# Order of early work in a local and pooled attention kernel with a cosine-gated FFN: loads, banks, sums of keys, and the first part of the passes

## The chip, the cores and the metric

The kernel runs on one core of a Trainium2 chip. Its engines are TensorE (PE in the profile; its weight loads are PEld), VectorE (DVE), ScalarE (ACT), GpSimd (POOL) and SyncE (SP, which issues most DMAs). SBUF holds tiles of 128 partitions, PSUM has eight banks that take matmul results. The metric is the device time of one execution in microseconds, less is better.

## The reference

Eight batches of eight heads with 576 tokens of width 64. Each head gets two attentions, which are added; then an FFN with `h * cos(h)` follows.

```python
q_d = q.reshape(B, H, Sd, factor, D).mean(axis=3)     # k_d, v_d alike; factor 4
out_up = np.repeat(sm_attn(q_d, k_d, v_d), factor, axis=2)
mask = np.abs(pos[:, None] - pos[None, :]) < factor
scores = np.where(mask, scale * np.matmul(q, k.transpose(0, 1, 3, 2)), -1000000000.0)
attn = softmax(scores)
out_local = np.matmul(attn, v)
x = (out_up + out_local).transpose(0, 2, 1, 3).reshape(B * S, H * D)
h = x @ w_in
g = h * np.cos(h)
return g @ w_out
```

`x` has 4608 rows of 512; `w_in` is 512 x 2048 and `w_out` 2048 x 512, both handed over in 64-bit floats, as two 32-bit words each.

## The kernel before

**Units.** Attention is done by pairs of heads: four pairs (`pr`) to a batch, 32 in all. A pair has five parts. `u_qk` loads q and k and sums them in groups of four tokens (`qkd`). `u_v` loads v twice, for the pooled attention (`vd4`, summed to `vd`) and for the local one (`vl`). `u_s` makes the scores on TensorE (L501 local, L509 pooled), masks them, takes maxima, exponentials and sums, and divides. `u_t` transposes the weights (L578, L589), and `u_pv` multiplies with the values (L606, L617), adds both attentions on VectorE (L625, the tile `xs`), and writes the result as a high and a low part (`x0h`, `x0l`, and so on) into x tiles of 384 tokens.

**FFN.** The tokens are 12 x tiles, d_ff is 16 chunks of 128. A step is one tile and one chunk: `gemm1` (12 matmuls, L668), an elementwise chain on ScalarE and VectorE whose first VectorE instruction is L680 and whose second is L683, and two steps later `gemm2` (9 matmuls, L704). There are 192 steps. `PASSES` gives their order: the first three tiles come with chunks 0 to 7, then the same three with chunks 8 to 15, then nine tiles with all chunks. The second part adds to the first in DRAM through GpSimd's DMA queue.

**Weights.** `w_load` brings a chunk of `w_in` or `w_out` as words (`wdi`, `wdo`, 512 KB each), and `w_split` makes a high and a low part: ScalarE L400, four VectorE instructions L401, L403, L405, L407 on a staging tile (`xxh` or `xxl`, with three places each), ScalarE's L411 and a subtraction (L379, on GpSimd or VectorE). 32 such splits are needed.

**Borrowed room.** The first two batches are early (`NEARLY`). Three of their four pairs work in the buffers of weight chunks 8 to 15 (`wx`, named wxi and wxo in the profile; `OWN` tells which); those chunks are loaded when the pairs are done. The last x tile lends the staging tiles.

**Order.** Nothing is placed by hand. `at(t, f, ...)` gives each part a due time, each operation has an estimated cost, and `Plan.schedule` lists the operations forwards and backwards over several rounds and keeps the best. Where an operation may run on two engines (`alts`), the planner picks one. Each engine then executes its own list in order. Where TensorE is expected to idle, matmuls on an identity (L806) are put in as filler. Early sums of keys (`ON_PE = (1,)`) are four matmuls with an identity (L455) and a copy (L440, L441); sums of queries are reductions on VectorE (L465) or three additions on GpSimd (L458, L460). `bank` gives the parts of batch 0 all eight banks; batch 1 uses the ring of three that the later batches use.

## Time and profile before

| | us |
|---|---|
| median of three runs | 1049.72 (1047.09 to 1053.25) |
| profiled execution | 1051.08 |
| its span | 1048.9 |
| TensorE busy in the span | 1015.9 |
| VectorE busy | 670.1 |
| ScalarE busy | 616.5 |
| GpSimd busy | 218.3 |

The profile cuts the span in 40 slices of 26.2 us and writes each engine's busy share in tenths. A line of a group or of the timeline names the engine, the source line, the operation and the tiles (result `<-` operands), then durations, and behind `<-` what ended the idle time ahead of it. A busy TensorE need not be at its peak, since matmuls overlap and filler counts as work. DMA moved 71.43 MB in the span.

### The profile page before, as it was taken

Reading aid. Unit: us, or ns where it says so; the run is one execution under the profiler, and the core shown is the slowest. Engines: PE = TensorE matmul, PEld = TensorE weight load, DVE = VectorE, ACT = ScalarE, POOL = GpSimd, SP = SyncE. Lnnn points to the kernel's source line nnn. Section 1 sums busy time; section 2 is a strip of 40 time slices with the busy share of each in tenths; the row PEclk is TensorE's granted clock in tenths of the full one; section 3 lists DMA queues with packets and bytes.
Section 4 is the critical chain, followed back from the end, with each engine's and each line's share of the span. In section 5 each row is a group of like instructions: output and inputs, shape, how many; then the busy total and the mean of one; then the engine's idle time right before and its main releaser. Section 6 shows DMA issues by size and latency. Waiting matters only on the chain.

```text
span 1048.9 us, 26356 instructions
## 1 busy us (share of the span) xinstructions
PE 1015.9 (97%) x11316; PEld 895.1 (85%) x11316; DVE 670.1 (64%) x1378; ACT 616.5 (59%) x1185; POOL 218.3 (21%) x225
## 2 busy tenths in 40 slices
PE   7987898999999999999999999999999999999998
PEld 6776787798888888888898888888898888899997
DVE  4698999964668766654647856745545964534433
ACT  2475776755566665665656755646656665555554
POOL 3557645311123211100102210300010210000000
PEclk8699899999999999999999999999999999999999
DMA  8385550002232411200102410300100410000000
GB/s 249 129 250 160 177 193 12 31 31 44 65 82 73 112 46 50 81 24 28 54 28 70 119 43 24 108 24 27 54 28 24 131 55 1 31 1 1 31 1 31
DMA packets 33861, 71.43 MB, mean 68 GB/s; under 512 B 3152, under 2 KB 11344, under 8 KB 33744
## 3 DMA queue, kind: packets, MB, share of 16 engines
q1 hardware_dynamic: 32448, 67.38, 20.5%
q0 software_dynamic: 1296, 2.36, 1.6%
q8 instruction: 89, 1.46, 0.6%
q14 instruction: 28, 0.23, 0.1%
HBM read 57.93 MB, written 11.80 MB: 66 GB/s over the span
## 4 chain that ended last, share of the span: by engine, by line
PE 82%; DVE 11%; issue 2%; DMA 2%; ACT 1%; POOL 0%; SPq 0%; ACTq 0%; POOLq 0%; DVEq 0%
PE bank L704 34%; PE bank L668 33%; PE bank L617 4%; PE bank L501 3%; PE bank L509 2%; PE bank L606 2%; PE bank L589 2%; PE bank L455 1%; DMA wdi<-w_in 1%; PE bank L578 1%; PE bank L806 1%; DMA q<-qT 1%; DVE gl L379 1%; DVE tr L680 1%; DVE xxl L405 1%
## 5 line engine op out<-in xcount | busy, mean ns | idle before, releaser
L704 PE MATMUL bank<-wo,gh 128*128 128x512 f32 x1152 | 366.8, 399 | 0.6 <-DVE ob L721 0.6
L704 PEld LDWEIGHTS bank<-wo,gh 128*128 128x128 f32 x1152 | 210.0, 189 | 37.1 <-issue 3.3
L704 PE MATMUL bank<-wo,gl 128*128 128x512 f32 x576 | 228.9, 398 | 0.9 <-DVE gl L379 0.9
L683 DVE SCALAR_TENSOR_TENSOR tr<-tr,bank 128x384 f32<-128x384 f32 x192 | 105.6, 550 | 130.4 <-ACT tr L678 130.2
L679 ACT ACTIVATE tr<-bank,bmagic 128x384 f32<-128x384 f32 x192 | 110.8, 577 | 123.8 <-PE bank L668 116.7
L680 DVE SCALAR_TENSOR_TENSOR tr<-tr,bank 128x384 f32<-128x384 f32 x192 | 105.7, 551 | 101.5 <-ACT tr L679 101.4
L677 ACT ACTIVATE tr<-tr 128x384 f32<-128x384 f32 x192 | 100.8, 525 | 94.7 <-DVE tr L680 93.9
L685 ACT ACTIVATE gh<-tr 128x384 fp32r<-128x384 f32 x171 | 89.6, 524 | 104.9 <-DVE tr L683 103.5
L379 DVE TENSOR_TENSOR gl<-tr,gh 128x384 fp32r<-128x384 f32 x157 | 96.7, 616 | 72.8 <-ACT gh L685 71.1
L704 PEld LDWEIGHTS bank<-wo,gl 128*128 128x128 f32 x576 | 108.6, 189 | 25.8 <-DVE gl L379 1.7
L668 PE MATMUL bank<-x1h,wi 128*128 128x384 f32 x384 | 108.0, 342 | 3.4 <-DVE tr L683 3.4
L668 PE MATMUL bank<-x0h,wi 128*128 128x384 f32 x384 | 108.4, 343 | 1.5 <-DVE tr L683 1.5
L668 PE MATMUL bank<-x2h,wi 128*128 128x384 f32 x384 | 106.8, 338 | 0.9 <-DVE tr L683 0.9
L668 PE MATMUL bank<-x3h,wi 128*128 128x384 f32 x384 | 107.1, 339 | 0.0
L678 ACT ACTIVATE tr<-tr 128x384 f32<-128x384 f32 x192 | 100.9, 526 | 6.1
L379 POOL TENSOR_TENSOR gl<-tr,gh 128x384 fp32r<-128x384 f32 x35 | 38.1, 1090 | 317.8 <-DVE gh L686 256.9
L668 PEld LDWEIGHTS bank<-x1h,wi 128*128 128x128 f32 x384 | 70.9, 190 | 6.7 <-DVE tr L683 4.7
L668 PEld LDWEIGHTS bank<-x0h,wi 128*128 128x128 f32 x384 | 70.9, 190 | 4.8 <-DVE tr L683 2.4
L668 PEld LDWEIGHTS bank<-x2h,wi 128*128 128x128 f32 x384 | 70.2, 188 | 3.5 <-DVE tr L683 1.4
L668 PEld LDWEIGHTS bank<-x3h,wi 128*128 128x128 f32 x384 | 70.2, 188 | 2.3 <-issue 0.4
L668 PE MATMUL bank<-x1l,wi 128*128 128x384 f32 x192 | 65.0, 339 | 0.0
L668 PE MATMUL bank<-x0l,wi 128*128 128x384 f32 x192 | 64.9, 338 | 0.0
(190 smaller groups left out, 1513.1 us busy)
## 6 DMA issues: line engine op xcount, KB each, us to landing
...
```

The source lines that it names most:

```text
L379: f = lambda e: lambda: e.tensor_tensor(out=out(), in0=in0(), in1=in1(), op=ALU.subtract)
L501: pe.matmul(banks[h].get()[BS * i:BS * (i + 1), LQ + BS * s:LQ + BS * (s + 1)], q.get()[hs, o:o + BS], k.get()[hs, o:o + BS], start=True, ...
L509: pe.matmul(banks[h].get()[:HD, i * SD:(i + 1) * SD], qkd.get()[hs, 0, i * HD:(i + 1) * HD], qkd.get()[hs, 1, :], start=True, stop=True)
L617: pe.matmul(banks[e].get()[64 * h:64 * h + 64, o:o + BQ], vt.get()[r, a, i, :], ptl.get()[r, a, i, :], start=True, stop=True)
L668: pe.matmul(ph.get()[:, :m], w[:, i, kc, :], x[:, kc, :], start=(n == 0), stop=(n == 3 * KC - 1))
L677: act.activation(tr.get(), tr.get(), AF.Sin, scale=PI)
L678: act.activation(tr.get(), tr.get(), AF.Square)
L679: pl.op("ACT", _act(m, True, 1), lambda: act.activation(tr.get(), h(), AF.Identity, bias=bmagic), r=[ph], w=[tr])
L680: pl.op("DVE", _dve(m), lambda: dve.scalar_tensor_tensor(out=tr.get(), in0=tr.get(), scalar=MAGIC, in1=h(), op0=ALU.subtract, op1=ALU.subt ...
L683: pl.op("DVE", _dve(m), lambda: dve.scalar_tensor_tensor(out=tr.get(), in0=tr.get(), scalar=0.5, in1=h(), op0=ALU.subtract, op1=ALU.mult), ...
L685: pl.op("ACT", _act(m, False), lambda: act.activation(gh.get(), tr.get(), AF.Copy), r=[tr], w=[gh], alts=[("DVE", _dve(m / 2), lambda: dve ...
L704: pe.matmul(o, (gh, gh, gl)[k].get()[:, sl], wo.get()[:, (0, 1, 0)[k]], start=(c == c0 and k == 0), stop=(c == c1 - 1 and k == 2))
```

## The change

1. `PASSES` has chunks 0 to 3 (`NF = 4`) in the first part on three tiles, then chunks 4 to 15.
2. `ON_PE = ()`: early sums of keys are made as the sums of queries are, on VectorE or GpSimd.
3. Batch 1 uses all eight banks as batch 0 does, its parts are due earlier, and batches 0 and 1 get a lead of 100 and 60 us in the planner's keys (`BOOST`).
4. A chain of dependencies puts the loads of the two batches and of all weights into one order. Queries and keys of batch 1's pairs get buffers of their own (in `xxl` and in chunks 6 to 8).
5. For that, `w_split` stages in `xxh` alone, with three places.
6. The sums of both softmaxes lie in one tile `su`, so that the small addition and the reciprocal are one instruction each for both; GpSimd sets `su` to one first.

```diff
-PASSES = [(t, 0, NC // 2) for t in range(3)] + [(t, NC // 2, NC) for t in range(3)] + [(t, 0, NC) for t in range(3, NT)]
+NF = 4
+PASSES = [(t, 0, NF) for t in range(3)] + [(t, NF, NC) for t in range(3)] + [(t, 0, NC) for t in range(3, NT)]
-ON_PE = (1,)
+ON_PE = ()
+BOOST = {0: 100.0, 1: 60.0}
...
-            span, rev = self.run({o: -o.fin for o in self.ops}, True)
-            key = {o: (1 - CFG["mix"]) * (span - o.fin) + CFG["mix"] * key[o] for o in self.ops}
+            span, rev = self.run({o: o.boost - o.fin for o in self.ops}, True)
+            key = {o: span - o.fin - o.boost for o in self.ops}
...
-    for c in range(NC - 8, NC):
+    for c in range(NC - 10, NC):
...
-        v = cut(xx[nstage[0] % 2], DM * (nstage[0] // 2 % 3), [P, DM])
+        v = cut(xx[0], DM * (nstage[0] % 3), [P, DM])
...
+        if b == 1 and pr and name in "qk":
+            own = cut(xx[1], 584 * (name == "k"), shape) if pr == 1 else \
+                cut(wx[{(2, "q"): ("o", 8), (2, "k"): ("i", 7), (3, "q"): ("o", 7), (3, "k"): ("o", 6)}[(pr, name)]], 0, shape)
+            return own
...
-        if b == 0:
+        if b < NEARLY:
...
-            pl.op("DVE", 0.1, lambda su=su: dve.tensor_scalar(out=su.get(), in0=su.get(), scalar1=1e-9, scalar2=2.0 * PI,
-                                                              op0=ALU.add, op1=ALU.mult), w=[su])
-            pl.op("DVE", 0.15, lambda su=su: dve.reciprocal(su.get(), su.get()), w=[su])
+        pl.op("DVE", 0.1, lambda: dve.tensor_scalar(out=su.get(), in0=su.get(), scalar1=1e-9, scalar2=2.0 * PI,
+                                                    op0=ALU.add, op1=ALU.mult), r=[su2], w=[su])
+        pl.op("DVE", 0.15, lambda: dve.reciprocal(su.get(), su.get()), w=[su])
...
-            t = need[c] if c < NC // 2 else NC // 2 + 2.0 * (c - NC // 2)
+            t = need[c] if c < NF else NF + c - NF
...
-        for t, f in ((-4.0 + 0.5 * i, u_qk), (-2.4 + 0.5 * i, u_v), (0.1 + 1.5 * i, u_s), (1.4 + 1.5 * i, u_t), (2.7 + 1.5 * i, u_pv)):
+        for t, f in ((-7.9 + 0.5 * i, u_qk), (-4.4 + 0.5 * i, u_v), (-3.4 + i, u_s), (-2.4 + i, u_t), (-1.4 + i, u_pv)):
             at(t, f, 1, i)
...
+    chain = [o for k in ul("u_qk", 0) + ul("u_v", 0) + ul("u_qk", 1) + wl(0) + ul("u_v", 1) + wl(*range(1, NC))
+             for o in loads[k]]
+    for o, n in zip(chain, chain[1:]):
+        n.sdeps.append(o)
```

In the changed kernel the line numbers shift: L501 becomes L513, L509 L521, L578 L595, L589 L606, L606 L623, L617 L634, L625 L642, L668 L685, L680 L697, L683 L700, L704 L721, L806 L835, L379 L386, the split's L400 to L411 become L407 to L418.

What the planner makes of it is seen at three places. On TensorE, at the start, behind the first filler (k and q are pair 0 of batch 0; wxo_120 and wxi_151 hold pair 1), before:

```order
L455 MATMUL bank<-k,ident 128x144 x4
L501 MATMUL bank<-k,q 32x32 x48
L509 MATMUL bank<-qkd 72x144 x4
L455 MATMUL bank<-wxo_120,ident 128x144 x4
L501 MATMUL bank<-wxo_120,wxi_151 32x32 x48
L509 MATMUL bank<-wxi_151 72x144 x4
L455 MATMUL bank<-wxi_208,ident 128x144 x4
L455 MATMUL bank<-wxo_211,ident 128x144 x4
```

and in the changed kernel, a little later, from the fourth pair's scores (wxo_287 and wxi_230) through the first pair's transposes and product with the values to the second pair's transpose:

```order
L513 MATMUL bank<-wxo_287,wxi_230 32x32 x48
L521 MATMUL bank<-wxi_230 72x144 x4
L595 MATMUL bank<-ident,sml 128x128 x3
L606 MATMUL bank<-ident,smd 72x72 x8
L634 MATMUL bank<-ptl,vl 64x24 x48
L623 MATMUL bank<-ptd,vd 64x144 x4
L595 MATMUL bank<-ident,wxi_291 128x128 x3
```

The matmuls with keys are gone, and pairs follow each other without them. On SyncE, from the loads that follow those of batch 0, before:

```order
L390 DMA wdi_544<-w_in 128x4x256 [waits DMAHW0_49]
L390 DMA wdo_613<-w_out 128x1024 [waits DMAHW1_49]
L451 DMA q<-qT 128x584 [waits DMAHW2_49,DVE_49,PE_49]
L451 DMA wxo_120<-kT 128x584 [waits DMAHW3_49,PE_49,Activation_49]
L390 DMA wdi_729<-w_in 128x4x256 [waits DMAHW4_49]
L451 DMA k<-kT 128x584 [waits DMAHW5_49]
L451 DMA wxi_208<-kT 128x584 [waits DMAHW6_49,PE_49,Activation_49]
L390 DMA wdo_833<-w_out 128x1024 [waits DMAHW7_49]
```

and now (xxl and the wx tiles with numbers from 725 on are batch 1's own buffers for q and k):

```order
L463 DMA q<-qT 128x584 [waits DMAHW0_49,DVE_49,PE_49]
L463 DMA k<-kT 128x584 [waits DMAHW1_49,DVE_49]
L463 DMA xxl<-qT 128x584 [waits DMAHW2_49]
L463 DMA xxl<-kT 128x584 [waits DMAHW3_49]
L463 DMA wxo_725<-qT 128x584 [waits DMAHW4_49]
L463 DMA wxi_790<-kT 128x584 [waits DMAHW5_49]
L463 DMA wxo_803<-qT 128x584 [waits DMAHW6_49]
L463 DMA wxo_866<-kT 128x584 [waits DMAHW7_49]
L397 DMA wdi_930<-w_in 128x4x256 [waits DMAHW0_49]
L397 DMA wdo_954<-w_out 128x1024 [waits DMAHW1_49]
L484 DMA vd_1032<-vdn 72x1024 [waits DMAHW2_49,DVE_49]
L485 DMA vl<-vl 128x768 [waits DMAHW3_49,PE_49]
```

Keys and queries of batch 1 no longer wait for ScalarE or TensorE, except those of pair 0; weights of chunk 0 stand behind them, and all other weights behind batch 1's values. On VectorE, between step 0's second instruction (L683, L700) and the next step's first (L680, L697), before:

```order
L683 SCALAR_TENSOR_TENSOR tr<-tr,bank 128x384
L407 SCALAR_TENSOR_TENSOR xxl<-wdi_972,xxl 128x512
L680 SCALAR_TENSOR_TENSOR tr<-tr,bank 128x384
L401 TENSOR_SCALAR xxh<-xxh 128x512
L401 TENSOR_SCALAR xxl<-xxl 128x512
L560 TENSOR_REDUCE sul<-wxi_292 128x12
L562 TENSOR_SCALAR sud<-sud 72x4
```

and now:

```order
L700 SCALAR_TENSOR_TENSOR tr<-tr,bank 128x384
L408 TENSOR_SCALAR xxh<-xxh 128x512
L412 SCALAR_TENSOR_TENSOR xxh<-wdo_1322,xxh 128x512
L410 TENSOR_SCALAR xxh<-xxh 128x512
L414 SCALAR_TENSOR_TENSOR xxh<-wdo_1322,xxh 128x512
L412 SCALAR_TENSOR_TENSOR xxh<-wdi_1365,xxh 128x512
L408 TENSOR_SCALAR xxh<-xxh 128x512
L386 TENSOR_TENSOR wo_1884<-xxh,wo_1884 128x512
L414 SCALAR_TENSOR_TENSOR xxh<-wdi_1365,xxh 128x512
```

Parts of pairs stood among the first steps before (L560, L562 here); now splits of weights, all staged in `xxh`, stand there, and the pairs are ahead of them.

More of the change, by code (lines that the diff above doesn't have):

```diff
@@ L72 @@
     __slots__ = ("eng", "dur", "fn", "tab", "deps", "sdeps", "now", "start", "end", "lat", "name", "arg", "preds", "succs",
-                 "i", "fin", "bank", "alts")
+                 "i", "fin", "bank", "alts", "boost")
 class Plan:
@@ L81, in __init__ @@
         self.ops, self.rings, self.turns, self.bufs, self.now, self.log, self.name, self.arg = [], {}, {}, [], 0.0, [], "", ()
-        self.banks = []
+        self.banks, self.boost = [], 0.0
     def buf(self, make, tag=None):
@@ L217, in run @@
                 heapq.heappop(ready[e])
+            t = max(t, avail[o][e])
             dur = o.alts[e][0]
@@ L370, in attn_ffn_kernel @@
               "o": w_out.bitcast(I32).rearrange("f (n t) -> f n t", t=2)}
+    loads = {}
     def dma(nbytes, fn, r=(), w=(), pw=()):
-        return pl.op("SP", max(0.45, nbytes / 262e3), fn, r=r, w=w, pw=pw, lat=1.8)
+        o = pl.op("SP", max(0.45, nbytes / 262e3), fn, r=r, w=w, pw=pw, lat=1.8)
+        loads.setdefault((pl.name,) + pl.arg, []).append(o)
+        return o
     nstage = [0]
@@ L448, in u_qk @@
         early = b < NEARLY
-        bk = bank(b, "t") if early else None
+        bk = bank(b, "t") if early and ON_PE else None
         for i, (src, ram) in enumerate(((q, qT), (k, kT))):
@@ L511, in u_s @@
         pl.op("PE", 0.65, d_mm, r=[qkd], pw=banks, w=poo)
-        mxl, sul = sb("mxl", 2, [P, 2 * NSEG]), sb("sul", 2, [P, 2 * NSEG])
+        mxl, su = sb("mxl", 2, [P, 2 * NSEG]), sb("su", 2, [P, 2 * NSEG + 4])
+        sul = lambda: su.get()[:, :2 * NSEG]
+        sud = lambda: su.get()[:HD, 2 * NSEG:].rearrange("p (a b) -> p a b", a=2)
+        pl.op("POOL", 0.15, lambda: pool.memset(su.get(), 1.0), w=[su])
         s5 = lambda: sml.get().rearrange("p (a h e) n -> p a h e n", a=NSEG // 2, h=2)
@@ L536, in u_s @@
                     r=[poo[h], mx], pw=[smd]))
-        m = 4 * SD
-        bd = lambda t: t.get().unsqueeze(3).broadcast_to([HD, 2, 2, SD])
+        m, su2 = 4 * SD, pl.buf(None)
+        bd = lambda t: t.unsqueeze(3).broadcast_to([HD, 2, 2, SD])
         if early:
@@ L548, in exps @@
                         act.activation(smd.get()[:, h, i], dq(h)[:, i], AF.Exp, bias=mxd.get()[:, h, i:i + 1], scale=1.0 / 128.0,
-                                       accum_out=sud.get()[:, h, i:i + 1])
-            o = pl.op("ACT", _act(n, False) + 4 * (_act(SD, True, 2) + 0.1), exps, r=[mxd] + poo, w=[sml, smd, sud], tab="exp")
+                                       accum_out=sud()[:, h, i:i + 1])
+            o = pl.op("ACT", _act(n, False) + 4 * (_act(SD, True, 2) + 0.1), exps, r=[mxd, su] + poo, w=[sml, smd], pw=[su2], tab="exp")
             for bk in banks:
@@ L557, in u_s @@
             pl.op("ACT", _act(n, False) + _act(m, False), exps, w=[sml, smd], tab="exp")
-        for sm, su, size, bc in ((sml, sul, n, bl), (smd, sud, m, bd)):
-            if not (early and su is sud):
-                pl.op("DVE", _dve(size), lambda sm=sm, su=su: dve.tensor_reduce(out=su.get(), in_=sm.get(), axis=AX.X, op=ALU.add),
-                      r=[sm], w=[su])
-            pl.op("DVE", 0.1, lambda su=su: dve.tensor_scalar(out=su.get(), in0=su.get(), scalar1=1e-9, scalar2=2.0 * PI,
-                                                              op0=ALU.add, op1=ALU.mult), w=[su])
-            pl.op("DVE", 0.15, lambda su=su: dve.reciprocal(su.get(), su.get()), w=[su])
-            f = lambda e, sm=sm, su=su, bc=bc: lambda: e.tensor_tensor(out=sm.get(), in0=sm.get(), in1=bc(su), op=ALU.mult)
+        for sm, part, size in ((sml, sul, n), (smd, sud, m)):
+            if not (early and sm is smd):
+                pl.op("DVE", _dve(size), lambda sm=sm, part=part: dve.tensor_reduce(
+                    out=part(), in_=sm.get(), axis=AX.X, op=ALU.add), r=[sm, su], pw=[su2])
+        pl.op("DVE", 0.1, lambda: dve.tensor_scalar(out=su.get(), in0=su.get(), scalar1=1e-9, scalar2=2.0 * PI,
+                                                    op0=ALU.add, op1=ALU.mult), r=[su2], w=[su])
+        pl.op("DVE", 0.15, lambda: dve.reciprocal(su.get(), su.get()), w=[su])
+        for sm, part, size, bc in ((sml, sul, n, bl), (smd, sud, m, bd)):
+            f = lambda e, sm=sm, part=part, bc=bc: lambda: e.tensor_tensor(out=sm.get(), in0=sm.get(), in1=bc(part()), op=ALU.mult)
             pl.op("POOL", _pool(size), f(pool), r=[su], w=[sm], alts=[("DVE", _dve(size), f(dve))])
@@ L777, in attn_ffn_kernel, with wl, ul @@
         pl.now, pl.arg = t, a
+        pl.boost = BOOST.get(a[0], 0.0) if f in (u_qk, u_v, u_s, u_t, u_pv) else 0.0
         f(*a)
+    def wl(*cs):
+        return [("w_load", k, c) for c in cs for k in "io"]
+    def ul(f, b):
+        return [(f, b, i) for i in range(NPAIR)]
+    chain = [o for k in ul("u_qk", 0) + ul("u_v", 0) + ul("u_qk", 1) + wl(0) + ul("u_v", 1) + wl(*range(1, NC))
+             for o in loads[k]]
+    for o, n in zip(chain, chain[1:]):
+        n.sdeps.append(o)
     order = pl.schedule()
```

8 lines of the change are left out of this document (4 added, 4 removed).

## The prediction

> **What bounds the kernel now.** I read the page first, then a table of three stretches that I cut at two instructions of VectorE, then the waits and the timeline inside the first two.
>
> ```profile
> span 1048.9 us, 26356 instructions
> PE   7987898999999999999999999999999999999998
> DVE  4698999964668766654647856745545964534433
> ```
>
> In the slices (26.2 us each) TensorE is full from the ninth on and VectorE is full from the third to the eighth. So two regimes follow each other. The border is found with the first elementwise instruction of each matmul step (L680; a step is one tile and one chunk, 192 in all):
>
> ```profile
> 67.29 0.54 DVE L680 SCALAR_TENSOR_TENSOR tr<-tr,bank 128x384 f32<-128x384 f32 x1
> 218.25 0.55 DVE L680 SCALAR_TENSOR_TENSOR tr<-tr,bank 128x384 f32<-128x384 f32 x1
> 1039.08 0.55 DVE L680 SCALAR_TENSOR_TENSOR tr<-tr,bank 128x384 f32<-128x384 f32 x1 [0.78 <-ACT tr L679]
> ...
> 1011.21 2.10 PE bank L668 x12
> 1013.31 2.08 PE bank L704 x9
> 1015.39 2.10 PE bank L668 x12
> ```
>
> These are steps 0, 24 and 191. On the chain of waits a step late in the kernel takes 1015.39 - 1011.21 = 4.18 us of TensorE and nothing else. From step 24 to 191 are 167 steps, 698 us, and 820.8 us pass; the other 123 us are 24 pairs of heads at 5.1 us, about what their matmuls take. TensorE has nothing left to lose there. What comes ahead of step 24 can still shrink:
>
> ```profile
> core 0: us, PE busy (x) PEld busy (x) DVE busy (x) ACT busy (x) POOL busy (x), PEclk, DMA share, GB/s
> 0.00:67.30 67.30, 60.18 (x1209) 52.18 (x1210) 42.88 (x112) 28.93 (x90) 30.01 (x43) 0.82 0.63 193
> 67.30:218.25 150.95, 132.25 (x1446) 112.85 (x1445) 144.28 (x248) 103.69 (x209) 87.51 (x72) 0.95 0.39 123
> 218.25:1048.90 830.65, 823.44 (x8666) 730.10 (x8664) 482.89 (x1021) 483.89 (x887) 100.82 (x111) 1.00 0.17 48
> ```
>
> From step 0 to step 24 VectorE is busy for 144.3 of 151.0 us: it is the bound, and 24 steps that TensorE could do in 100 us take 151. Ahead of step 0 VectorE idles for 24.4 us and the first batch's chain of latencies is the bound. So the span is **T24** (the start of the 25th L680) plus a rest of 830.65 us, and T24 is **T0** (67.3) plus a VectorE-bound stretch (151.0).
>
> **The change part by part.** *Sums of keys.* For eight early pairs TensorE summed keys by identity matmuls (L455), and ScalarE or VectorE copied them out:
>
> ```profile
> by line: PE bank L455 23.0%; DMA wdi<-w_in 13.4%; PE bank L617 10.3%; PE bank L806 9.5%; PE bank L606 6.2%; issue 5.6%; PE bank L501 4.7%; PE bank L589 4.3%; PE bank L509 3.7%; DVE wxi L565 3.0%; PE bank L578 3.0%; SPq L390 1.6%; DVE sud L5
> ...
> 44.80 2.33 PE bank L455 x8
> ...
> L465 DVE TENSOR_REDUCE qkd<-q 128x144 f32<-128x576 f32 x1 | 0.8, 753 | 3.6 <-DMA q<-qT 3.6
> ```
>
> The first line is the chain of waits of the first 67.3 us by line: 23.0%, 15.5 us, is L455, in line with all else. It goes. In its place come reductions of 0.75 us; the program's order gives VectorE 8 of the 16 early query and key sums (it had 4) and GpSimd the others, so the change does only half of what its name says. What is late next is VectorE itself. Also on that chain stand 13.4%, 9.0 us, of waiting for a weight chunk, because SyncE had been held up:
>
> ```profile
> SPq L451 <- PE bank L606: 36.5, 3, 20.4
> SPq L390 <- PE bank L617: 16.7, 1, 16.7
> SPq L390 <- DVE wxi L625: 11.0, 1, 11.0
> ```
>
> SyncE's queue stood for 36.5 + 16.7 + 11.0 us behind single loads that needed a buffer. *Fixed order of loads*, with buffers of their own for the second batch's queries and keys: the weights of chunk 0 now stand ahead of the waiting loads, so the 9.0 us should go too. But rows 27 to 34 (the second batch's values) still wait for the first batch's results, and all other weights queue behind them. I cost this at nothing, since chunks 1 to 3 are wanted only at T0; if the cover fails, that is, if the first batch ends late, T0 moves with it anyway.
>
> *Both batches first.* T0 now stands behind eight pairs and not four. The first batch's pairs leave VectorE at
>
> ```profile
> 33.14 0.82 DVE L625 TENSOR_TENSOR xs<-bank,xd 128x288 f32<-128x288 f32 x2 [0.56 <-ACT xd L440]
> 39.08 0.82 DVE L625 TENSOR_TENSOR wxi<-bank,wxi 128x288 f32<-128x288 f32 x2 [2.42 <-POOL qkd L458]
> 45.22 0.46 DVE L625 TENSOR_TENSOR wxo<-bank,wxo 128x288 f32<-128x288 f32 x1 [2.90 <-issue]
> ```
>
> 6 us apart until L455 returns at 44.8. Taking both items off the chain, 67.3 - 15.5 - 9.0 = 42.8 us for four pairs and the first gemm; four more at 6 us give T0 = 67. That is the lower estimate. As a check, VectorE's own work ahead of step 0: in the order 136 attention rows and 10 of the weight split, counted by kind at the timeline's start-to-start times (0.67 for a key sum, 0.36 for a 288-wide row, 0.46 for a 384-wide one, and so on), are 54 us; the same count for before gives 40, where 42.9 were busy. Before, 64% of that stretch was busy; at 64% the 54 (58 with the same surplus) would need 91 us. Between 67 and 91 I take **T0 = 76**, nearer to the first, since the key matmuls and the hold-ups that made the 64% are what goes; both ends are kept.
>
> *The split's share after T0.* Of the VectorE rows between step 0 and step 24, 245 become 211: attention rows move ahead of T0, and 30 weight splits (before 27) are left. In start-to-start times,
>
> ```profile
> 39.82 0.42 DVE L401 TENSOR_SCALAR xxh<-xxh 128x512 f32<-128x512 f32 x1
> 40.16 0.68 DVE L405 SCALAR_TENSOR_TENSOR xxl<-wdi,xxl 128x512 int32<-128x512 int32 x1
> 40.76 0.42 DVE L403 TENSOR_SCALAR xxh<-xxh 128x512 int32<-128x512 int32 x1
> 41.09 0.69 DVE L407 SCALAR_TENSOR_TENSOR xxl<-wdi,xxl 128x512 int32<-128x512 int32 x1
> ...
> L405 DVE SCALAR_TENSOR_TENSOR xxh<-wdo,xxh 128x512 int32<-128x512 int32 x14 | 16.2, 1154 | 0.0
> ```
>
> a split is 0.34 + 0.60 + 0.33 + 0.60 = 1.9 us undisturbed; in the stretch its L405 alone averages 1.15. Undisturbed, before has 106 us of VectorE work here and after has 99. The 45 us between 106 and 151 are 6.7 us idle and 38 us by which instructions stretch while GpSimd works:
>
> ```profile
> 26.22 1.26 POOL L478 TENSOR_TENSOR wxo<-wxo 72x512 f32<-72x512 f32 x1
> 91.38 1.00 POOL L379 TENSOR_TENSOR gl<-tr,gh 128x384 fp32r<-128x384 f32 x1
> 92.34 1.30 POOL L379 TENSOR_TENSOR wo<-xxh,wo 128x512 fp32r<-128x512 f32 x1
> 93.60 4.44 POOL L478 TENSOR_TENSOR wxi<-wxi 72x512 f32<-72x512 f32 x1
> ...
> L478 POOL TENSOR_TENSOR vd<-vd 72x512 f32<-72x512 f32 x4 | 7.6, 1890 | 6.8 <-DMA vd<-vdn 6.8
> L478 POOL TENSOR_TENSOR wxi<-wxi 72x512 f32<-72x512 f32 x2 | 7.4, 3683 | 0.1
> ```
>
> (L478 takes 1.26 us alone and 4.44 beside the splits; the two engines hold each other up). Seven value sums of pairs fell into this stretch, and six of them (the two groups) took 15.0 us in this first of their two instructions alone; the order now has five of the seven ahead of T0, and two key or query sums besides: some 16 of GpSimd's 87.5 us. So I scale the 38 by 99/106 and by 0.82: 29 us. With the same 6.7 idle the stretch is 99 + 29 + 6.7 = **135 us**. Bounds: 101 with no stretching and hardly any idle, 157 by the rival on staging below.
>
> [...]
>
> *Smaller edits.* Two small instructions on sums become one of each (9 fewer L562 and 9 fewer L564 by step 24, under 4 us together, counted above). The first part of the passes (chunks 0 to 3 on three tiles) makes the last chunk due at step 23, before it was step 31; VectorE's order has the last split at step 24 in both, so no step is freed by it. By step 24 one more pair's second half is done, three groups of matmuls of 0.45, 1.59 and 0.71 us:
>
> ```profile
> 53.22 0.45 PE L589 MATMUL bank<-ident,wxi 72*72 72x72 f32 x4 [0.22 <-ACT wxi L440]
> 53.59 1.59 PE L617 MATMUL bank<-wxi,wxo 32*64 32x24 f32 x96
> 55.12 0.71 PE L606 MATMUL bank<-wxo 72*64 72x144 f32 x8
> ```
>
> The rest shrinks by those 2.7 us to 828.0.
>
> *Sum.* T24 = 76 + 135 = 211 (before 218.25). The span is 211 + 828 = 1039 us. The profiled execution took 1051.08, 2.2 us more than its span, and stood 1.4 above the median of the three runs (1049.72); on the scale of the median the forecast is 1039 + 2.2 - 1.4 = **1040 us**, 0.9% less.
>
> **The rivals.**
>
> 1. *The eight pairs run dense.* T0 = 67, and with fewer operations on GpSimd the stretch takes 125: T24 = 192, span 1020, time **1021**. For it: the 6 us spacing; against it: in-order queues filled with two batches.
> 2. *The second batch does not overlap with the first.* In before its pairs came slowly,
>
> ```profile
> 92.19 0.45 DVE L625 TENSOR_TENSOR xs<-bank,xd 128x288 f32<-128x288 f32 x1
> 131.66 0.81 DVE L625 TENSOR_TENSOR wxi<-bank,wxi 128x288 f32<-128x288 f32 x2
> ```
>
> 39 us for the last three of them, 13 each. In the order the score matmuls of five of the eight pairs still wait for ScalarE, that is, for banks that an earlier pair holds. With T0 = 86, T24 is 221 and the time **1050**: no change.
> 3. *Staging* (the other side). The split's staging tile has three places, before it had six. A split may start only when the third one before it has been subtracted. One such life in before runs from ScalarE's L400 to GpSimd's L379:
>
> ```profile
> 34.22 0.65 ACT L400 ACTIVATE xxl<-wdi 128x512 f32<-128x512 f32 x1
> 46.27 4.20 POOL L379 TENSOR_TENSOR wi<-xxl,wi 128x512 fp32r<-128x512 f32 x1 [2.18 <-ACT wi L411]
> ```
>
> 16 us, most of it lying about. 29.5 splits on three places need 29.5 x 16 / 3 = 157 us if lives stay so long: T24 = 233, time **1062**, slower. It decides from a life of 15.2 us on (a stretch of 149). Against it: 1.9 us of VectorE work, two ScalarE and one GpSimd instruction add up to 5 us, so lives of 10 are possible.
> [...]
>
> **How the numbers follow.** Forecast (1031 to 1044.5) 0.40, rival 1 (below) 0.22, rival 2 (1044.5 to 1055) 0.21, rivals 3 and 4 (above) 0.10 and 0.07. A run of this kernel can tell changes of about 0.5% from none, 5.2 us; so faster 0.62, same 0.21, slower 0.17. The range that leaves out 0.2 runs from rival 1 to just above rival 2: 1021 to 1056.
>
> **What would show it.** In the new profile: no identity matmuls ahead of the first step; step 0's L697 at 70 to 84 us; step 24's at 204 to 217, with VectorE over 90% busy in between; its L412 below 1.1 us in the mean; the rest after it 828 us. A first L697 after 86, or ScalarE's L407 waiting for subtractions by many microseconds in total, would make the forecast wrong.

## The result: slower by half a per cent, and the profile after

| us | before | after | forecast |
|---|---|---|---|
| median (11 runs each) | 1052.69 | 1058.21 | 1040 |
| span of the profiled execution | 1048.9 | 1054.7 | 1039 |
| T0, step 0's first VectorE instruction | 67.3 | 91.4 | 76 |
| T0 to step 24 | 151.0 | 134.1 | 135 |
| step 24 to the end | 830.65 | 829.2 | 828 |

The ratio after to before is 1.0056 (95% interval 1.0031 to 1.0082). The range ended at 1056; the time lies above it, and on the side that had a chance of 0.17. A small part of the miss is the scale: the forecast stood on a time before of 1049.72 us (three runs), and eleven runs give 1052.69. Two of the three terms came within 1.2 us. T0 alone came 15 us late: 24 us are added ahead of step 0, and 17 are saved behind it.

The windows of the changed kernel, cut at the same two instructions (columns as before), and these two instructions on VectorE's timeline:

```profile
0.00:91.44 91.44, 74.79 (x1973) 64.44 (x1974) 62.90 (x145) 33.52 (x115) 45.40 (x77) 0.76 0.71 238
91.44:225.53 134.09, 120.66 (x892) 105.28 (x889) 129.04 (x213) 94.85 (x178) 57.32 (x48) 0.96 0.25 84
225.53:1054.70 829.17, 823.62 (x8589) 729.58 (x8587) 472.52 (x959) 490.75 (x902) 93.12 (x115) 1.00 0.16 46
...
91.44 0.54 DVE L697 SCALAR_TENSOR_TENSOR tr<-tr,bank 128x384 f32<-128x384 f32 x1
225.53 0.54 DVE L697 SCALAR_TENSOR_TENSOR tr<-tr,bank 128x384 f32<-128x384 f32 x1
```

VectorE now has 62.9 us of work ahead of step 0 (42.9 before), as the change meant. But it idles there for 28.5 us, more than the 24.4 of before: the stretch grew by more than what was moved into it. The chain of waits of these 91.4 us, by line, and pieces of it in order of time (start, duration):

```profile
by line: PE bank L634 19.7%; PE bank L835 19.5%; issue 16.7%; PE bank L513 9.8%; PE bank L623 8.9%; PE bank L521 7.6%; PE bank L606 6.9%; PE bank L595 5.0%; PE bank L685 2.3%; DVE smd L582 0.7%; DVE wxi L453 0.5%; DVE sml L582 0.5%; ACT ptl
...
7.80 4.22 issue
...
15.13 2.86 PE bank L835 x41
18.53 1.10 issue
...
21.91 1.84 issue
...
27.46 3.13 issue
...
36.38 2.70 PE bank L634 x96
...
53.70 1.16 PE bank L623 x8
...
56.03 2.99 PE bank L835 x27
...
72.84 1.64 PE bank L634 x96
```

Nearly all of it is TensorE. Its small attention matmuls (L634, L513, L623, L521, L606, L595) hold over half. 19.5%, 17.8 us, are filler (L835), which the planner had put where it expected TensorE to be idle. Whether the filler held up other work there, or only took the place of a wait, this profile doesn't tell. 16.7%, 15.3 us, are "issue": TensorE waited for nothing that the profile shows; before, that was 5.6% of 67.3, 3.8 us. The piece at 53.70 holds the last matmuls of batch 0's last pair. They end at 54.9 us, before at 55.8: 1 us earlier and not 24. The windows by 10 us show at what speed this ran:

```profile
30.00:40.00 10.00, 9.34 (x239) 7.89 (x239) 5.77 (x16) 3.15 (x12) 4.36 (x9) 0.50 0.15 47
40.00:50.00 10.00, 9.68 (x250) 7.87 (x234) 6.32 (x16) 2.59 (x7) 7.61 (x14) 0.50 0.26 73
50.00:60.00 10.00, 10.00 (x243) 8.80 (x242) 7.02 (x20) 4.81 (x16) 1.53 (x2) 0.50 0.62 189
```

TensorE is busy for 29.0 of 30 us and its granted clock is 0.50. Cut by 1 us, both profiles show 1.00 or 0.50 there, and something between only where the clock changes; so the means of 0.76 over 91.4 us and 0.82 over 67.3 us make 44 us at half clock ahead of step 0, and 24 before. A group of 96 L634 takes 2.70 us at half clock (at 36.38 above) and 1.64 later on at full clock (at 72.84).

### The profile page after: what moved, and what is told of

Same layout as the page of the kernel before. It is cut to its first block, busy times and chain, and to the rows that moved or that the text cites. A ratio compares the mean times of both kernels' runs of the same rounds, so it can differ in the third digit from the quotient of the medians.

```text
span 1054.7 us, 26617 instructions
## 1 busy us (share of the span) xinstructions
PE 1019.1 (97%) x11447; PEld 899.3 (85%) x11447; DVE 664.5 (63%) x1315; ACT 619.1 (59%) x1194; POOL 195.8 (19%) x239
## 4 chain that ended last, share of the span: by engine, by line
PE 86%; DVE 8%; issue 3%; ACT 1%; ACTq 0%; POOL 0%; POOLq 0%; DVEq 0%
PE bank L721 34%; PE bank L685 34%; PE bank L634 5%; PE bank L513 3%; PE bank L835 2%; PE bank L623 2%; PE bank L521 2%; DVE xxh L412 2%; PE bank L606 2%; DVE xxh L414 1%; DVE xxh L408 1%; PE bank L595 1%; DVE tr L697 1%; DVE xxh L410 1%; DVE tr L700 1%
## 5 line engine op out<-in xcount | busy, mean ns | idle before, releaser
L721 PE MATMUL bank<-wo,gh 128*128 128x512 f32 x1152 | 365.0, 398 | 0.1
L721 PEld LDWEIGHTS bank<-wo,gh 128*128 128x128 f32 x1152 | 208.8, 188 | 37.4 <-issue 4.0
L721 PE MATMUL bank<-wo,gl 128*128 128x512 f32 x576 | 228.2, 396 | 0.6 <-DVE gl L386 0.5
L700 DVE SCALAR_TENSOR_TENSOR tr<-tr,bank 128x384 f32<-128x384 f32 x192 | 105.8, 551 | 144.1 <-ACT tr L695 144.1
L697 DVE SCALAR_TENSOR_TENSOR tr<-tr,bank 128x384 f32<-128x384 f32 x192 | 105.7, 550 | 101.9 <-ACT tr L696 101.5
L386 DVE TENSOR_TENSOR gl<-tr,gh 128x384 fp32r<-128x384 f32 x163 | 92.9, 570 | 73.2 <-ACT gh L702 72.1
L721 PEld LDWEIGHTS bank<-wo,gl 128*128 128x128 f32 x576 | 108.0, 187 | 25.7 <-DVE gl L386 1.3
L685 PE MATMUL bank<-x0h,wi 128*128 128x384 f32 x384 | 108.6, 344 | 5.7 <-DVE tr L700 5.4
L685 PE MATMUL bank<-x2h,wi 128*128 128x384 f32 x384 | 106.9, 339 | 2.3 <-DVE tr L700 2.3
L685 PE MATMUL bank<-x1h,wi 128*128 128x384 f32 x384 | 106.8, 339 | 1.0 <-DVE tr L700 1.0
L685 PE MATMUL bank<-x3h,wi 128*128 128x384 f32 x384 | 106.9, 339 | 0.1
L386 POOL TENSOR_TENSOR gl<-tr,gh 128x384 fp32r<-128x384 f32 x29 | 32.5, 1122 | 313.7 <-DVE gh L703 250.3
L685 PEld LDWEIGHTS bank<-x0h,wi 128*128 128x128 f32 x384 | 71.1, 190 | 9.8 <-DVE tr L700 7.2
L685 PEld LDWEIGHTS bank<-x2h,wi 128*128 128x128 f32 x384 | 70.2, 188 | 5.1 <-DVE tr L700 2.4
L685 PEld LDWEIGHTS bank<-x1h,wi 128*128 128x128 f32 x384 | 70.2, 188 | 4.4 <-DVE tr L700 2.1
L685 PEld LDWEIGHTS bank<-x3h,wi 128*128 128x128 f32 x384 | 70.2, 188 | 2.7 <-issue 0.6
L685 PE MATMUL bank<-x0l,wi 128*128 128x384 f32 x192 | 65.2, 340 | 0.0
L685 PE MATMUL bank<-x3l,wi 128*128 128x384 f32 x192 | 64.5, 336 | 0.0
```

Source lines behind the costliest of these rows:

```text
L386: f = lambda e: lambda: e.tensor_tensor(out=out(), in0=in0(), in1=in1(), op=ALU.subtract)
L685: pe.matmul(ph.get()[:, :m], w[:, i, kc, :], x[:, kc, :], start=(n == 0), stop=(n == 3 * KC - 1))
L697: pl.op("DVE", _dve(m), lambda: dve.scalar_tensor_tensor(out=tr.get(), in0=tr.get(), scalar=MAGIC, in1=h(), op0=ALU.subtract, op1=ALU.subt ...
L700: pl.op("DVE", _dve(m), lambda: dve.scalar_tensor_tensor(out=tr.get(), in0=tr.get(), scalar=0.5, in1=h(), op0=ALU.subtract, op1=ALU.mult), ...
L721: pe.matmul(o, (gh, gh, gl)[k].get()[:, sl], wo.get()[:, (0, 1, 0)[k]], start=(c == c0 and k == 0), stop=(c == c1 - 1 and k == 2))
```

## The experiments

The theories after this reading: **clock** (without the dense key matmuls TensorE is at half clock for 44 us and not 24, and its chain is longer for it), **issue** (the early loads fill the DMA engines, and TensorE waits for instructions that come by the same engines: the page lists 90 instruction packets on them, and whose they are it doesn't say), **filler** (planned fillers stand on the chain). The planner makes a new order for every edit. T0, and the start of step 48, by which all versions have done the same steps (339.2 before, 344.2 after), tell more than a total. Both come from one profiled execution of each version. The changed kernel and the one with more transfers (below) run the same instructions up to 29 us and are 2.9 us apart there, so a difference in T0 of some 3 us is not read as an effect. Ratios are to the kernel before.

### One edit undone or taken out

**Key sums on TensorE again.**

```diff
-ON_PE = ()
+ON_PE = (1,)
```

> The changed kernel with the key sums of batches 0 and 1 back on TensorE (eight groups of four dense 128x128x144 matmuls), all else kept. Clock theory (without these dense matmuls TensorE stands at half clock for 44 us of the first 91, against 24 us of 67 before, and its chain is longer for it): time at half clock ahead of the first step falls to 25 us or less, step 0 starts at 76 to 82 us instead of 91.4, total 1042 to 1049. Issue theory (TensorE waits for its own instructions while the early loads fill the DMA engines, 15.3 us of the chain): nothing is relieved, eight groups of 0.5 to 0.9 us are added, step 0 at 92 to 98. Filler theory (planned filler matmuls of 17.8 us stand on the chain): step 0 within 4 us of 91.4.

**Loads in the planner's order.**

```diff
-    for o, n in zip(chain, chain[1:]):
-        n.sdeps.append(o)
```

> The changed kernel without the fixed order of loads (the planner orders them). Issue theory: stalls put down to issue ahead of step 0 fall from 15.3 us to 5 or less, step 0 starts at 79 to 83 us, total 1045 to 1050. Clock theory and filler theory: the clock and the fillers do not hang on the loads, step 0 within 4 us of 91.4, total within 5 us of the changed kernel's.

**No fillers.**

```diff
-           fgap=0.4, f0=0.8, fend=300.0)
+           fgap=0.4, f0=0.8, fend=0.0)
```

> The changed kernel without any filler matmul. Filler theory: the 17.8 us that fillers hold in the chain of waits ahead of step 0 go, step 0 starts at 73 to 77 us, total 1040 to 1045. Clock theory: fillers are by now the only dense matmuls ahead of step 0, so the half clock lasts longer than 44 us, and step 0 starts no earlier than 85 us, perhaps past 95. Issue theory: some 400 instructions fewer to fetch, issue falls by a few us, step 0 at 80 to 88.

**First part with eight chunks.**

```diff
-NF = 4
+NF = 8
```

> The changed kernel with the first part of the passes at chunks 0 to 7 again. All three theories place the loss ahead of step 0, which the passes do not touch: step 0 within 4 us of 91.4. The stretch of steps 0 to 23 then holds eight chunks' splits as before (151 us there, 134 after): step 24 stands 5 to 15 us later, the rest is shorter by up to as much, total 1055 to 1070. If the total came to 1050 or less, the smaller first part would be the loss instead.

| | T0 | half clock ahead of it | step 48 | median | ratio (interval) |
|---|---|---|---|---|---|
| keys on TensorE | 90.2 | 27 | 345.4 | 1053.80 | 1.0020 (0.9995 to 1.0046) |
| loads free | 90.5 | 54 | 339.8 | 1054.91 | 1.0022 (0.9997 to 1.0048) |
| no fillers | 87.2 | 64 | 338.8 | 1047.48 | 0.9954 (0.9925 to 0.9982) |
| eight chunks | 93.7 | 51 | 342.2 | 1052.14 | 1.0013 (0.9986 to 1.0041) |

No theory got the gain in T0 that it forecast for its own edit (clock 76 to 82, issue 79 to 83, filler 73 to 77). With the key matmuls the clock did come back (27 us at half clock, near the 24 of before), yet T0 stayed: in the chain the key matmuls stand in the place of what was gained. One of their groups takes 2.2 to 2.4 us, not the 0.5 to 0.9 of my expectation. With the loads free, issue holds 16.9% of 90.5 us, 15.3 as in the changed kernel, where 5 or less was expected. The chains of waits ahead of step 0, with key matmuls (L467) and without fillers:

```profile
by line: PE bank L467 19.2%; PE bank L835 13.9%; issue 13.4%; PE bank L634 11.3%; PE bank L513 9.2%; PE bank L521 6.9%; PE bank L623 4.8%; PE bank L606 4.6%; PE bank L595 4.4%; PE bank L685 4.3%; POOL wxi L490 2.5%; POOL wxo L491 1.6%; POOL
```

```profile
by line: PE bank L634 19.4%; issue 12.1%; PE bank L623 8.5%; PE bank L606 5.9%; PE bank L513 5.8%; DMA wxi<-qT 5.7%; PE bank L595 5.6%; PE bank L521 5.5%; POOL wi L386 3.1%; DVE mxd L547 2.8%; DVE wxo L492 2.1%; ACT wxi L564 1.8%; POOL qkd 
```

In the first, L467 has 17.3 us of 90.2 and L634 10.2 instead of 18.0. In the second, the 17.8 us of filler are gone and T0 is 4.3 us earlier, for loads, GpSimd and VectorE now stand in the chain, and the half clock lasts 64 us. It is the first version with a time below before, and T0 lay where the clock theory had it (85 or later) and the issue theory too (80 to 88). The eight chunks moved step 24 from 225.5 to 221.1, earlier and not later as I expected.

### The key sums alone, on the kernel before

**Before with `ON_PE = ()`** (and no bank taken for the key sums), **before without fillers**, and **both**:

```diff
-ON_PE = (1,)
+ON_PE = ()
...
-        bk = bank(b, "t") if early else None
+        bk = bank(b, "t") if early and ON_PE else None
```

> The kernel before with the key sums of batches 0 and 1 on VectorE and GpSimd instead of TensorE, nothing else changed. The prediction's step (15.5 us of the chain ahead of step 0 are these matmuls, and go): step 0 starts at 52 to 56 us instead of 67.3, total 1036 to 1043. Replacement theory (the chain up to the first softmax waits for loads and for TensorE's own instructions, planned fillers take the place of these matmuls, and without them the clock stands lower): step 0 at 62 to 68, time at half clock up from 24 to 35 us or more, total within 5 us of before.

> The kernel before without filler matmuls. If fillers on the chain were a cost that the change alone brought in (11.2 us busy before, 20 after), before loses nothing without them: step 0 within 3 us of 67.3, total within 4 us. If the fillers cost either kernel alike, step 0 comes 4 us earlier here too (4.3 us in the changed kernel without them) and the total falls by 6 to 10 us.

> The kernel before with the key sums on VectorE and without fillers. With fillers, taking the key matmuls off TensorE moved step 0 by 0.6 us only (67.3 to 66.7), where the prediction had 15.5. If fillers alone took their place in the chain: step 0 at 52 to 57 us here (69.6 with key matmuls and without fillers). If it was the half clock and TensorE's waits for instructions: step 0 at 62 to 68, half clock 45 us or more of it, total 1046 to 1054.

| | T0 | step 24 | step 48 | median | ratio (interval) |
|---|---|---|---|---|---|
| keys off TensorE | 66.7 | 221.4 | 345.0 | 1056.45 | 1.0024 (0.9997 to 1.0051) |
| no fillers | 69.6 | 217.1 | 337.5 | 1049.55 | 0.9959 (0.9933 to 0.9984) |
| both | 64.2 | 217.6 | 338.9 | 1052.91 | 1.0010 (0.9979 to 1.0042) |

The first row decides: the 15.5 us of L455 are taken off the chain, and T0 moves by 0.6 us where 11 to 15 were expected. Step 24 comes no earlier at all (218.25 before): the key sums of the second batch now lie in the stretch behind T0, on GpSimd, whose sums of queries and keys take 29.5 us there (15.3 before). VectorE, busy for 151.1 of 154.7 us, is still the bound there. By step 48 this version is as late as the changed kernel (345.0 and 344.2). TensorE's timeline of that run shows what came in their place:

```profile
11.96 0.35 PE L501 MATMUL bank<-wxo,wxi 64*32 64x32 f32 x12 [3.65 <-issue]
12.25 2.10 PE L806 MATMUL bank<-ident_b 128*128 128x128 bf16 x18
14.28 1.24 PE L509 MATMUL bank<-wxi 64*72 64x144 f32 x8
15.45 3.44 PE L806 MATMUL bank<-ident_b 128*128 128x128 bf16 x41
...
26.76 0.47 PE L501 MATMUL bank<-wxo,wxi 64*32 64x32 f32 x31 [4.54 <-issue]
...
57.39 5.94 PE L806 MATMUL bank<-ident_b 128*128 128x128 bf16 x65
63.14 0.42 PE L668 MATMUL bank<-x0h,wi 128*128 128x384 f32 x1
...
0.00:66.70 66.70, 54.85 (x1184) 47.70 (x1185) 39.17 (x96) 25.14 (x80) 36.73 (x53) 0.67 0.70 226
```

Fillers stand where four groups of key matmuls stood (3.9 to 19.8 us before), waits for issue are longer (8.6 us for L501 ahead of 66 us, 4.2 before), the half clock lasts 44 us instead of 24, and at the end 65 fillers in a row stand ahead of the first gemm. Without fillers the key sums' removal is worth 5.5 us of T0 (69.6 to 64.2), and by step 24 nothing is left of it (217.6 and 217.1). There TensorE waits for others; its waits ahead of step 0:

```profile
PE bank L501 <- issue: 6.5, 2, 4.1
PE bank L501 <- DMA k<-kT: 4.6, 1, 4.6
PE bank L668 <- POOL x0l L379: 3.5, 1, 3.5
PE bank L617 <- issue: 2.2, 1, 2.2
```

The third is new: the first gemm waits for GpSimd, which got key sums (37.2 us busy ahead of step 0, and 34.6 with the key matmuls and without fillers) and subtracts the low part of the first x tile late.

The table also says what the fillers cost. Taking them out brings before to 0.9959 and the changed kernel to 0.9954, with intervals that overlap: without fillers, the whole change neither gains nor loses. With them the changed kernel is at 1.0056. So it is the fillers that make it slower than before, and they cost before 0.4% too, although T0 there came 2.3 us later without them.

### Where batch 1 stands

**Batch 1 late again**: the changed kernel with batch 1's old due times, no lead for it, and the old banks; that needs eight chunks and the planner's order of loads.

```diff
-NF = 4
+NF = 8
...
-BOOST = {0: 100.0, 1: 60.0}
+BOOST = {0: 100.0}
...
-        if b < NEARLY:
+        if b == 0:
             tags = {"s": ("pa.0", "po.0", "pa.1", "po.1"), "t": ("ph.0", "ph.1"), "v": ("pa.2", "po.2")}[kind]
...
-        for t, f in ((-7.9 + 0.5 * i, u_qk), (-4.4 + 0.5 * i, u_v), (-3.4 + i, u_s), (-2.4 + i, u_t), (-1.4 + i, u_pv)):
+        for t, f in ((-4.0 + 0.5 * i, u_qk), (-2.4 + 0.5 * i, u_v), (0.1 + 1.5 * i, u_s), (1.4 + 1.5 * i, u_t), (2.7 + 1.5 * i, u_pv)):
...
-    for o, n in zip(chain, chain[1:]):
-        n.sdeps.append(o)
```

> The changed kernel with batch 1 where it stood before (its places and priority, its pairs spread over steps -4 to 7, its banks those of later batches), which needs chunks 0 to 7 in the first part again and the loads in the planner's order; what stays of the change are the key sums on VectorE, the sums of the softmax in one tile and the staging in three places. If moving batch 1's four pairs ahead of step 0 is what costs (24 us: four pairs ended at 53.7 and the first step came at 91.4): step 0 at 58 to 66 us, the stretch to step 24 back at 145 to 155, step 48 within 4 us of 339, total 1045 to 1053. If the chain without the key matmuls were really 15 us shorter: step 0 at 50 to 56, total below 1043. If the loss lies in the new sums or the staging: step 0 near 62 and step 24 later than 222.

T0 is 74.6, step 24 at 222.9, step 48 at 344.6, the median 1057.12, ratio 1.0037 (1.0008 to 1.0065). The windows of this run, and those of the run with eight chunks and batch 1 early:

```profile
0.00:74.63 74.63, 58.11 (x1377) 51.28 (x1377) 51.68 (x106) 26.28 (x81) 38.20 (x63) 0.77 0.75 232
74.63:222.87 148.24, 132.03 (x1361) 113.09 (x1358) 143.95 (x242) 103.51 (x207) 87.75 (x75) 0.94 0.29 96
```

```profile
0.00:93.65 93.65, 75.80 (x2001) 65.63 (x2002) 65.11 (x140) 36.29 (x119) 47.37 (x78) 0.73 0.71 230
93.65:221.13 127.48, 116.13 (x762) 101.11 (x760) 122.11 (x210) 87.25 (x164) 59.64 (x47) 0.97 0.24 78
```

Moving batch 1 ahead adds 19.0 us to T0 and takes 20.8 from the stretch: near enough an exchange. And with batch 1 late, what stays of the change is no faster than before either. My expectation held for the stretch (145 to 155) and missed T0 (58 to 66), step 48 (within 4 us of 339) and the total (1045 to 1053). What stays also holds the new sums and the staging. Before with nothing but its key sums moved is as late at step 48 (345.0), so these two need have no part in it, but no run tests them alone.

### The clock

**Bursts of dense matmuls instead of fillers.** Without planned fillers, 40 matmuls of 128x128 at four places.

```diff
+BURST = [("u_pv", (0, 0)), ("u_pv", (0, 2)), ("u_s", (1, 2)), ("u_pv", (1, 1))]
...
+            if o.eng == "PE" and (o.name, o.arg) in BURST:
+                BURST.remove((o.name, o.arg))
+                s = spare(o.start - 0.3, o.start)
+                for _ in range(40):
+                    pe.matmul(s[2].get()[:, 0:P], ident_b, ident_b, start=True, stop=True)
```

> The changed kernel without its planned fillers (as in the run without filler matmuls: step 0 at 87.2, 65 us at half clock), but with four bursts of 40 dense 128x128 matmuls ahead of the tails of pairs 0 and 2 of batch 0, the scores of pair 2 and the tail of pair 1 of batch 1. Clock theory (small matmuls don't hold the clock up, a dense burst lifts it, and TensorE at half clock is the chain): time at half clock falls to 40 us or less, TensorE's rest ahead of step 0 is worth 12 us less, the bursts cost 9 to 13: step 0 at 82 to 88. Without the clock in the chain: the bursts alone are added, step 0 at 96 to 100, total 1054 to 1060.

By the clock column the half clock fell from 64 to 37 us. T0 is 88.5 (87.2 without bursts), the median 1052.13, ratio 0.9987 (0.9964 to 1.0009; 0.9954 without bursts). The bursts (L842) hold 12.9% of the chain of 88.45 us, 11.4 us. TensorE's order is otherwise the same in both versions, so the same matmuls can be compared, those of batch 0's last pair, without bursts and with them (source lines shift by one):

```profile
49.10 2.77 PE L634 MATMUL bank<-wxi,wxo 32*64 32x24 f32 x96
51.80 1.23 PE L623 MATMUL bank<-wxo 72*64 72x144 f32 x8
```

```profile
47.89 1.59 PE L635 MATMUL bank<-wxi,wxo 32*64 32x24 f32 x96
49.41 0.71 PE L624 MATMUL bank<-wxo 72*64 72x144 f32 x8
```

They take little more than half the time, and they end at 50.1 us where they ended at 53.0, although two bursts, 8.1 us, stand ahead of them. Some 11 us came back, then: 2.8 are shorter waits for issue (4.3 us up to there, and 7.1 without bursts), and some 8 are left for the clock. So the clock is in the chain. Ahead of step 0 as a whole the bursts returned about what they cost. My T0 for it (82 to 88) was just missed, and as a means it pays nothing.

**Fillers in the planned first 16 us only** (`fend=16.0`).

> The changed kernel with its fillers only in the planned first 16 us (93 of the 219 ahead of step 0). If the late fillers are the cost, step 0 starts at 86 to 89 us and the total falls by 8 to 11, as without any (87.2 and 1047.5). If the early ones are, step 0 stays at 90 to 93, total at 1053 or more.

T0 90.4, median 1053.75, ratio 1.0013 (0.9980 to 1.0047): the early fillers alone bring T0 back to that of the changed kernel, as I expected if they are the cost. They don't hold the clock up: by its column it is at half for 69 us ahead of step 0. Step 48 (341.5) lies between 338.8 without any filler and 344.2 with all, so the late ones cost something too.

### The waits for issue

**Batch 1's q and k held back** until the last scores of batch 0 are reduced, by a copy into the first of their tiles.

```diff
+        if (b, pr) == (1, 0):
+            late = st[(0, NPAIR - 1)]["mxl"]
+            pl.op("POOL", 0.1, lambda: pool.tensor_copy(q.get()[:, 0:1], late.get()[:, 0:1]), r=[late], w=[q])
...
-        for t, f in ((-7.9 + 0.5 * i, u_qk), (-4.4 + 0.5 * i, u_v), (-3.4 + i, u_s), (-2.4 + i, u_t), (-1.4 + i, u_pv)):
+        for t, f in ((-4.45 + 0.01 * i, u_qk), (-4.4 + 0.5 * i, u_v), (-3.4 + i, u_s), (-2.4 + i, u_t), (-1.4 + i, u_pv)):
```

> The changed kernel with the q and k loads of batch 1 held back until the scores of batch 0's last pair are reduced (a copy of one column into the first of their tiles waits for it), so that the DMA engines are not full ahead of 30 us; they were a quarter busy from 30 to 50. If TensorE's waits for instructions come of the loads that fill the DMA engines: the four stalls ahead of 31 us (10.3 us) fall to 5 or less, the first pair's tail ends at 24 to 27 us instead of 31.4, step 0 at 84 to 89. If the loads have nothing to do with it: the stalls stay at 8 to 12 us, and step 0 at 90 to 96, later if batch 1's scores then wait for their loads.

**More transfers**, 16 of 256 KB from an idle tile to output rows that are written over later, where the DMA engines had little to do.

```diff
+    spill = []
...
+            if o.eng == "ACT" and 20.0 < o.start < 44.0 and len(spill) < 16:
+                spill.append(o)
+                act.dma_start(out[NTOK - P * len(spill):NTOK - P * len(spill) + P, :].rearrange("p (a n) -> p a n", a=4),
+                              ident.unsqueeze(1).broadcast_to([P, 4, P]))
```

> The changed kernel with 16 more transfers of 256 KB each, from an idle tile to rows of the output that are written over later, issued by ScalarE between its instructions from the first softmax on (some 25 to 60 us). If full DMA engines make TensorE wait for its instructions: in the stretch from 30 to 60 us, where such waits were 0.3 us and the DMA engines 15 to 62% busy, they come to 4 us or more, and step 0 comes at 95 us or later. If not: they stay below 1.5 us there, and step 0 within 3 us of 91.4.

Held back, the DMA engines are 2% busy from 20 to 30 us (88% in the changed kernel) and the waits ahead of 31 us fall from 10.3 to 3.7 us (3.39 and 0.31). They come back where the loads went: from 30 to 50 us the DMA share is 0.94 and 0.63, and two waits of 2.25 and 2.39 us stand there, against one of 0.32 that began there in the changed kernel. In all, issue has 18.4% of 90.2 us, 16.6, and neither the end of the first pair's L634 (29.9 us, and not 24 to 27) nor T0 (90.2, and not 84 to 89) comes where it should if the loads are all (median 1055.38, ratio 1.0035, 0.9997 to 1.0073). With more transfers the order of TensorE's instructions is the same, so single places can be compared. The first place is the 36th matmul of the third pair's L634, in the changed kernel and with the transfers, with the window around it (DMA is the next to last number):

```profile
44.83 1.91 PE L634 MATMUL bank<-wxo,wxi 32*64 32x24 f32 x61 [0.32 <-issue]
...
40.00:50.00 10.00, 9.68 (x250) 7.87 (x234) 6.32 (x16) 2.59 (x7) 7.61 (x14) 0.50 0.26 73
```

```profile
48.43 1.91 PE L634 MATMUL bank<-wxo,wxi 32*64 32x24 f32 x61 [1.70 <-issue]
...
40.00:50.00 10.00, 7.74 (x317) 6.88 (x315) 5.96 (x14) 2.18 (x6) 7.53 (x14) 0.50 0.75 212
```

The wait falls on the same matmul and is five times as long at three times the traffic. But it goes the other way at the 79th matmul of the first pair's L634, again in the changed kernel and with the transfers, with the first of the added transfers:

```profile
26.11 1.35 PE L634 MATMUL bank<-ptl,vl 32*64 32x24 f32 x78
30.59 0.83 PE L634 MATMUL bank<-ptl,vl 32*64 32x24 f32 x18 [3.13 <-issue]
```

```profile
29.01 2.34 PE L634 MATMUL bank<-ptl,vl 32*64 32x24 f32 x78
31.99 0.83 PE L634 MATMUL bank<-ptl,vl 32*64 32x24 f32 x18 [0.65 <-issue]
...
29.43 0.62 ACTq L841 DMA_DIRECT2D out<-ident  x1
```

Over all places ahead of step 0 the waits come to 14.7 us in either run. T0 is 95.0, as expected if the traffic counts (95 or later; single time 1060.2), but of these 3.6 us more, 2.9 were there when this L634 began, at 29.01 and not 26.11, ahead of the first added transfer. So single waits are longer at some places and shorter at others, and the runs don't show that the traffic makes the chain longer. From 30 to 60 us the waits came to 2.9 us (0.65, 0.57, 1.70), between the two expectations. Nor is traffic all that sets the length: in the changed kernel without fillers and in that with bursts one such wait, on the same matmul at a DMA share of 1.03 and 1.01, took 4.94 and 1.82 us.

What is shown is where the waits fall. Counted along TensorE's timeline, they come after 222, 348, 474, 602, 983, 1362, 1489 and 1617 matmuls in the changed kernel, after 222, 348, 474 and 983 in before with the key sums moved, and after 346, 474 and 855 in that without fillers. These are nearly the same counts, some 127 or a multiple of it apart, whatever matmuls stand there. That fits instructions that arrive in blocks, and the page lists a queue of instruction packets on the DMA engines; that the waits are for these packets is inferred:

```profile
q8 instruction: 90, 1.47, 0.6%
```

### Versions that beat both

**Key sums on TensorE and no fillers**, then that with eight chunks, and with the loads free (edits as above).

> The changed kernel with the key sums on TensorE and without fillers: the first two and third of the edits tried so far on it, together. If the key matmuls hold the clock up (27 us at half clock with them, 44 without) and the fillers are then 12.5 us of the chain for nothing: step 0 at 78 to 84 us, step 48 at 334 to 338, total 1040 to 1046, below both kernels. If fillers, keys and half clock only take each other's place: step 0 at 86 to 90, total 1046 to 1053.

> Key sums on TensorE, no fillers (1045.7, 0.994 of before) and the first part at chunks 0 to 7 again. If the smaller first part costs (undone alone on the changed kernel, the total came 0.4% lower): total 1040 to 1044, step 48 at 333 to 336. If not: 1044 to 1049, step 0 within 4 us of 86.

> Key sums on TensorE, no fillers and the loads in the planner's order. If the fixed order costs (undone alone on the changed kernel, the total came 0.3% lower): total 1040 to 1044, step 0 at 80 to 84. If not: 1044 to 1049, step 0 within 4 us of 86.

| | T0 | step 48 | median | ratio (interval) |
|---|---|---|---|---|
| keys on TensorE, no fillers | 86.0 | 337.0 | 1045.68 | 0.9942 (0.9909 to 0.9975) |
| and eight chunks | 87.0 | 337.3 | 1045.75 | 0.9944 (0.9923 to 0.9964) |
| and loads free | 90.8 | 340.6 | 1052.25 | 1.0019 (0.9998 to 1.0040) |

The first is the fastest measured, 0.6% below before and not by much ahead of before without fillers (0.9959). Its gain was not the sum of its parts (T0 78 to 84 expected). The number of chunks makes no difference on it. Undoing the fixed order of loads costs 0.8% on it, though on the changed kernel that lowered the total by 0.3%. As the planner makes a new order each time, these runs don't tell an edit's own effect of that size from that of the new order.

## Why the prediction was wrong, step by step

- **Two regimes, and the span as T0, stretch and rest: right.** Stretch 134.1 (135), rest 829.2 (828).
- **The split's share and the stretching by GpSimd: right in sum.** VectorE was busy 129.0 of 134.1 us. Both groups of the split's L412 in the stretch,

```profile
L412 DVE SCALAR_TENSOR_TENSOR xxh<-wdo,xxh 128x512 int32<-128x512 int32 x15 | 16.5, 1102 | 0.0
L412 DVE SCALAR_TENSOR_TENSOR xxh<-wdi,xxh 128x512 int32<-128x512 int32 x15 | 14.8, 987 | 0.0
```

  average 1.04 us (below 1.1 was asked for). ScalarE's L407 waited for subtractions for 7.0 us in ten waits, so staging did hold it up at times; but VectorE idled for 5.0 us in all, and the 157 us of the staging rival did not come. Rival 4, at 0.07, had all of GpSimd's forecast 48 us added to VectorE's 99 and the idle 6.7, a stretch of 154 us and a time of 1059. No run shows such a sum: with the 57.3 us that GpSimd worked in this stretch it would have been 163 us, and 134.1 came. What the profile shows is that single instructions stretch: L412 takes 0.67 to 0.69 us where GpSimd is idle, and up to 1.77 beside it.
- **T0, the failed step.** The step is the subtraction 67.3 - 15.5 - 9.0 = 42.8 us: it took the shares that two items have in a chain of waits for time that goes with them. The key sums' removal alone brought 0.6 us (5.5 without fillers), the 9.0 us were not ahead of step 0 at all (below), and batch 0's last pair ended 1 us earlier and not 24. In the place of what was taken off came fillers, longer waits for issue, half clock and GpSimd's late low part. How much each holds can't be added up, since they cover one another: taking out 17.8 us of filler brought 4.3, and putting 11.4 us of bursts in left T0 within the scatter. How the 15 us divide among them stays open. The other half of the sum, 24 us for four more pairs, fits: from 66.7 (before with the key sums moved) to 91.4 (all of the change) are 24.7 us, though all the other edits lie between the two, and moving batch 1 alone gave 19.0.
- **"What is late next is VectorE itself": wrong.** TensorE is late next. VectorE stayed at 69% of the stretch ahead of step 0 (64% before), and the check by utilisation, which gave 91, was the better estimate, in part by luck, since VectorE was not what bounds. That TensorE was busy for 60.2 of the 67.3 us, and VectorE for 42.9, stood in the quoted windows. I set the check aside with the argument that the key matmuls and hold-ups made the 64%; the run with the key sums alone denies it.
- **The 9 us of waiting for chunk 0's load: misread.** A chain taken for a window ends with the window's last instruction. That was not step 0's L680 but the split of a later chunk on ScalarE. In before, the chain's last pieces and TensorE's first gemm are

```profile
57.91 8.99 DMA wdi<-w_in
66.98 0.70 ACT xxl L400
...
62.28 0.42 PE L668 MATMUL bank<-x0h,wi 128*128 128x384 f32 x1
```

  The load ends when the first gemm has been running for over 4 us, so it cannot have held step 0 up, and there was nothing to gain from it. Of SyncE's three holds in the prediction, those of 16.7 and 11.0 us end behind step 0 too. The fixed order neither made nor cured the loss: without it T0 is 90.5.
- **The rivals.** The one nearest to what happened is the second, that the second batch's pairs lengthen the stretch ahead (T0 86, "no change"); it gave banks as the reason, and the runs show TensorE's own chain. Rivals 3 and 4 named times as near (1062 and 1059), but for a stretch of 157 or 154 us that came at 134.1. My list had no rival in which TensorE slows down when its dense matmuls leave (from 24 to 44 us at half clock in before with the key sums moved), although the clock column stood in the quoted windows (0.82).

With the measured T0 in the prediction's sum, 91.4 + 135 + 828 + 0.8, the time is 1055: the mechanism of exchange was right, and its price ahead of step 0 was not.
